# Decode attention on two kv heads at a time: 32 KB load rows, probabilities stationary, V moving

## The chip, the cores and the metric

The kernel runs on one core of a Trainium2 chip. The metric is the device time of one execution in microseconds (us). Two kernels are compared by the ratio of the mean time of one kernel's fast runs to the mean of the other's fast runs of the same rounds, so it is not quite the ratio of the medians that are quoted beside it. Traces and pages come from one profiled execution per kernel.

## The reference, cut to what matters

Eight sequences decode one token each through a modulated attention block and a gated feed-forward block. Nearly all bytes are the K and V caches: 8 x 4 kv heads x 8192 keys x 128 values in bfloat16, 2.1 MB for one K or V of one head, 134 MB in all. The weights add 51 MB.

```python
B, Hq, Hkv, Sk, Dh = 8, 32, 4, 8192, 128         # 8 query heads share a kv head
q = (h @ wq).reshape(B, 1, Hq, Dh)
scores = einsum('bhqd,bhkd->bhqk', q, repeat(k_cache, 8)) * Dh ** -0.5
p = softmax(scores)
o = einsum('bhqk,bhkd->bhqd', p, repeat(v_cache, 8))
x = x + ga * (o @ wo)        # then layernorm, gate and up, ReLU gate, down
```

## The kernel before

All loads go through one list in program order into an arena of nine slots of 2 MB (16 KB per partition). A load takes the next stretch of the arena when everything in it has been read in program order, and SyncE then waits on the chip for those reads:

```python
def pump():
    while stream:
        key, src, n = stream[0]
        lo = cursor[0] if cursor[0] + n <= NSLOT * SLOT else 0
        if P.unread("arena", lo, lo + n):
            return
        ...
        P.op("sp", lambda e, dst=dst, src=src: e.dma_start(dst, src), writes=[slot_r(lo, lo + n)], dma=True)
...
for n in range(N):           # 32 kv heads, one 2 MB load of K and one of V each
    load(("k", n), A_k_cache[n // G, n % G].rearrange("(p c) d -> p (c d)", p=128), SLOT)
    load(("v", n), A_v_cache[n // G, n % G].rearrange("(p c) d -> p (c d)", p=128), SLOT)
```

For each kv head VectorE transposes K in 32x32 blocks (four parts), TensorE makes the scores (QK, 16 matmuls of N = 512), the maximum of each query head is found, ScalarE takes the exponential, VectorE turns the probabilities, and TensorE multiplies with V. In this product V is the stationary operand and eight columns of probabilities move:

```python
for cc in range(NC):         # 64 matmuls of N = 8 per kv head
    fns.append(lambda e, cc=cc: e.matmul(ps[:, 3, col:col + J], vv[:, cc, :], pv_[:, cc % 16, cc // 16, :],
                                         start=(cc == 0), stop=(cc == NC - 1)))
```

The head loop is software-pipelined: K of head n+1 is transposed while the scores of head n and PV of head n-1 are made.

## Time and profile before

| | before |
|---|---|
| median time | 445.77 us (445.73 to 446.13, 4 runs) |
| span of the profiled run | 444.1 us |
| bytes read | 185.6 MB, 418 GB/s over the span |
| busy: PE, DVE, ACT | 66%, 49%, 7% |
| the last load has landed | 440.0 us |

How to read it: DMA engines are full in 38 of 40 slices while no compute engine is busy for more than two thirds of the time. So the question for any change is what it does to the stream of loads: how long a byte takes on its engine, and whether the engines always have a next load waiting. The lines are in the prediction.

### The profile page before, as it was taken

How to read it: one execution, taken by the hardware profiler on the slowest of the kernel's cores; microseconds unless marked ns; L12 is line 12 of the kernel's file. 1: busy time of each engine (PE TensorE's matmuls, PEld its weight loads, DVE VectorE, ACT ScalarE, POOL GpSimd, SP SyncE). 2: the span in 40 equal slices, each digit the busy share in tenths (PEclk: the TensorE clock that was granted, in tenths of full speed). 3: DMA queues.
4: the chain of work that ended last, by engine and by line, in shares of the span. 5: the costliest groups of instructions: out<-in, count | busy, mean ns of one | idle time of the engine just before them, and what ended most of it. 6: DMA issues, size and time to landing. Idle time of an engine off the chain costs nothing.

```text
span 444.1 us, 7822 instructions
## 1 busy us (share of the span) xinstructions
PE 290.9 (66%) x3514; PEld 165.4 (37%) x3514; DVE 217.7 (49%) x333; ACT 33.2 (7%) x78; POOL 30.8 (7%) x141
## 2 busy tenths in 40 slices
PE   0235355677858676776877767786777787558753
PEld 0111022344434333443433334343333345348741
DVE  0503065666655566666555566665556664230000
ACT  0200010000001000000100000001000002000000
POOL 4000020100000001000000110000001000000000
PEclk9995576887788888879688888778888869655555
DMA  8999999999999999999999999999999999999993
GB/s 344 421 428 425 434 434 428 426 429 437 427 428 432 431 426 426 435 434 425 426 434 429 425 429 435 429 425 432 429 430 428 429 421 403 422 430 429 426 429 151
DMA packets 16770, 186.14 MB, mean 419 GB/s; under 512 B 1537, under 2 KB 1633, under 8 KB 5985
## 3 DMA queue, kind: packets, MB, share of 16 engines
q1 hardware_dynamic: 16704, 185.64, 98.5%
q8 instruction: 27, 0.44, 0.4%
q14 instruction: 7, 0.05, 0.0%
q10 hardware_dynamic: 32, 0.01, 0.0%
HBM read 185.63 MB, written 0.02 MB: 418 GB/s over the span
## 4 chain that ended last, share of the span: by engine, by line
DMA 83%; PE 8%; DVE 7%; issue 1%; ACT 0%; SPq 0%; POOL 0%; DVEq 0%; ACTq 0%; POOLq 0%
DMA arena<-in_A_k_cache_dram 62%; DMA arena<-in_B_W_down_dram 8%; DMA arena<-in_A_wq_dram 7%; DMA arena<-in_A_wo_dram 4%; PE ps L460 4%; DVE kt L411 3%; DMA c_r<-in_c_dram 2%; PE ps L528 1%; DVE pT L450 1%; PE ps L334 1%; PE ps L420 1%; PE ps L357 0%; DVE lu L281 0%; ACT L278 0%; DVE hT L286 0%
## 5 line engine op out<-in xcount | busy, mean ns | idle before, releaser
L411 DVE STREAM_TRANSPOSE kt<-arena 128x1024 uint32<-128x1024 uint32 x128 | 153.3, 1218 | 114.6 <-DMA arena<-in_A_k_cache_dram 114.6
L420 PE MATMUL ps<-kt,qpad 128*128 128x512 bf16 x512 | 161.5, 482 | 2.0 <-POOL qpad L400 2.0
L420 PEld LDWEIGHTS ps<-kt,qpad 128*128 128x128 bf16 x512 | 60.9, 119 | 91.8 <-issue 60.6
L460 PE MATMUL ps<-pT,arena 128*128 128x8 bf16 x2048 | 56.0, 166 | 49.2 <-DVE pT L450 49.2
L460 PEld LDWEIGHTS ps<-pT,arena 128*128 128x128 bf16 x2048 | 54.1, 96 | 63.6 <-issue 63.3
L400 POOL COPY qpad<-qR 32x32 bf16<-32x32 bf16 x128 | 26.0, 203 | 312.8 <-PE ps L420 256.0
L430 PE MATMUL ps<-identf,negm 128*128 128x128 f32 x64 | 20.2, 408 | 37.0 <-DVE negm L426 37.0
L444 ACT ACTIVATE prb<-ps,bias 128x512 bf16<-128x512 f32 x32 | 22.0, 687 | 283.9 <-DVE mjt L438 283.9
L528 PE MATMUL ps<-hT,arena 128*128 128x8 bf16 x448 | 24.8, 194 | 7.7 <-DMA arena<-in_B_W_up_dram 3.0
L528 PEld LDWEIGHTS ps<-hT,arena 128*128 128x128 bf16 x448 | 24.4, 153 | 8.1 <-DMA arena<-in_B_W_up_dram 3.2
L430 PEld LDWEIGHTS ps<-identf,negm 128*128 128x128 f32 x64 | 12.3, 240 | 40.3 <-DVE negm L426 40.3
L450 DVE STREAM_TRANSPOSE pT<-prb 128x512 bf16<-128x512 bf16 x32 | 21.5, 672 | 1.7 <-ACT prb L444 1.7
L426 DVE TENSOR_REDUCE negm<-ps 128x1 f32<-128x512 f32 x32 | 20.9, 653 | 1.0 <-PE ps L420 1.0
L535 DVE TENSOR_TENSOR hmT<-ps,grel 128x224 bf16<-128x224 f32 x1 | 0.4, 391 | 30.7 <-ACT grel L533 30.7
L357 PE MATMUL ps<-arena,hT 128*32 128x512 bf16 x64 | 7.6, 627 | 11.2 <-DMA arena<-in_A_wq_dram 8.4
L303 PE MATMUL ps<-st,sel 128*128 128x1 f32 x4 | 1.2, 362 | 19.3 <-DVE st L302 19.3
L334 PE MATMUL ps<-arena,hT 128*32 128x512 bf16 x96 | 9.0, 544 | 6.8 <-DMA arena<-in_w_mod_dram 6.8
L545 PE MATMUL ps<-arena,hmT 128*32 128x256 bf16 x112 | 7.1, 415 | 7.4 <-DMA arena<-in_B_W_down_dram 7.4
L509 PE MATMUL ps<-arena,oT 128*32 128x256 bf16 x128 | 6.4, 382 | 5.2 <-DMA arena<-in_A_wo_dram 2.6
L341 DVE COPY mod<-ps 128x512 f32<-128x512 f32 x2 | 1.3, 670 | 15.2 <-PE ps L334 15.2
L436 DVE TENSOR_REDUCE mj<-ps 128x8 f32<-128x128 f32 x32 | 8.1, 252 | 1.2 <-PE ps L430 1.2
L303 PEld LDWEIGHTS ps<-st,sel 128*128 128x128 f32 x4 | 1.0, 310 | 19.6 <-DVE st L302 19.6
(64 smaller groups left out, 66.0 us busy)
## 6 DMA issues: line engine op xcount, KB each, us to landing
arena<-in_A_k_cache_dram SPq DMA_DIRECT2D x32, 2048.0 KB, 25.7
arena<-in_A_v_cache_dram SPq DMA_DIRECT2D x32, 2048.0 KB, 30.2
arena<-in_w_mod_dram SPq DMA_DIRECT2D x4, 3072.0 KB, 18.2
arena<-in_A_wq_dram SPq DMA_DIRECT2D x4, 2048.0 KB, 35.0
arena<-in_A_wo_dram SPq DMA_DIRECT2D x4, 2048.0 KB, 19.1
arena<-in_B_W_gate_dram SPq DMA_DIRECT2D x4, 1792.0 KB, 24.2
arena<-in_B_W_up_dram SPq DMA_DIRECT2D x4, 1792.0 KB, 28.0
arena<-in_B_W_down_dram SPq DMA_DIRECT2D x3, 1792.0 KB, 33.8
```

What stands on the lines that cost most here:

```text
L334: fns.append(lambda e, w=w, pr=pr, j=j, kk=kk: e.matmul(ps[32 * j:32 * j + 32, pr, :], hT[:, kk, :], w[:, 2 * pr:2 * pr + 2, j, :], start= ...
L357: fns.append(lambda e, w=w, z=z, g=g, kk=kk: e.matmul(ps[32 * g:32 * g + 32, 3 + z, :], hT[:, kk, :], w[:, g, z, :], start=(kk == 0), stop ...
L400: P.op("pool", lambda e, n=n, Q=Q: e.tensor_copy(qpad[32 * Q:32 * Q + 32, n % NQ, :, 24 + 32 * Q:32 + 32 * Q], qR[32 * Q:32 * Q + 32, :, n ...
L411: P.op("dve", lambda e: e.transpose(ktb[:, to:to + QE].bitcast(dt.uint32), arena[:, lo:lo + QE].bitcast(dt.uint32)), reads=[slot_r(lo, lo ...
L420: fns.append(lambda e, t=t, r=r: e.matmul(ps[:, n % 2, :].rearrange("p (c k) -> p c k", k=32), qpad[:, n % NQ, t * 2 + r, 24 - 8 * i:152 - ...
L426: P.op("dve", lambda e: e.tensor_reduce(negm[:, n % 2:n % 2 + 1], ps[:, n % 2, :], AX.X, ALU.max, negate=True), reads=[bank(n % 2)], write ...
L430: P.op("pe", lambda e: e.matmul(ps[:, 2, 0:128], negm[:, n % 2:n % 2 + 1].to_broadcast([128, 128]), identf[:], start=True, stop=True), rea ...
L436: P.op("dve", lambda e: e.tensor_reduce(mj[:, z, :], ps[:, 2, 0:128].rearrange("p (m j) -> p j m", j=J), AX.X, ALU.min), reads=[bank(2)], ...
L444: P.op("act", lambda e: e.activation(prb[:, z, :], ps[:, z, :], ACT.Exp, bias=bias[:, z:z + 1], scale=scale, accum_out=lall[:, n:n + 1]), ...
L450: P.op("dve", lambda e: e.transpose(pT[:, z, :], prb[:, z, :]), reads=[R("prb", z, z + 1)], writes=[R("pT", z, z + 1)])
L460: fns.append(lambda e, cc=cc: e.matmul(ps[:, 3, col:col + J], vv[:, cc, :], pv_[:, cc % 16, cc // 16, :], start=(cc == 0), stop=(cc == NC ...
L528: fns.append(lambda e, w=w, f=f, kk=kk, off=off, first=first: e.matmul(ps[:, 0, off + f * B:off + (f + 1) * B], w[:, f // FR, f % FR, :], ...
```

## The change

The intent is to handle two kv heads together: K and V of a pair come as one load of 4 MB with rows of 32 KB, half the partitions for each head. In PV the probabilities become the stationary operand (64 columns, zeros off the head's own block) and V moves with N = 512, in two column tiles side by side (matmuls that use one half each of TensorE's columns). The wanted 8-row diagonal blocks are then picked out and added by VectorE (the fold). The diff, cut to its core:

```diff
-        ktb = sb("kt", [128, 2 * SLOT], dt.bfloat16)
+        ktb = sb("kt", [128, 6 * 2048], dt.bfloat16)
-        for n in range(N):
-            load(("k", n), A_k_cache[n // G, n % G].rearrange("(p c) d -> p (c d)", p=128), SLOT)
-            load(("v", n), A_v_cache[n // G, n % G].rearrange("(p c) d -> p (c d)", p=128), SLOT)
+        for m in range(M):
+            for nm, t in (("k", A_k_cache), ("v", A_v_cache)):
+                load((nm, m), t[m // 2, 2 * (m % 2):2 * (m % 2) + 2].rearrange("g (p c) d -> (g p) (c d)", p=64), 2 * SLOT)
...
+            for t in range(32):
+                fns.append(lambda e, t=t: e.matmul(
+                    ps[64 * (t % 2):64 * (t % 2) + 64, 5, :].rearrange("p (i d) -> p i d", d=Dh),
+                    pT[:, z, t].rearrange("p g x -> p (g x)"), vv[:, t // 16, t % 16], start=(t < 2), stop=(t >= 30),
+                    tile_position=(0, 64 * (t % 2))))
...
+        def fold(m):
+            P.op("dve", lambda e: e.tensor_scalar(out=om[:], in0=ps[:, 5, 0:Dh], scalar1=im[:, 0:1], scalar2=None, op0=ALU.mult), ...)
+            for i in range(1, 4):
+                P.op("dve", lambda e, i=i: e.scalar_tensor_tensor(
+                    out=om[:], in0=ps[:, 5, Dh * i:Dh * i + Dh], scalar=im[:, i:i + 1], in1=om[:], op0=ALU.mult, op1=ALU.add), ...)
...
+        for m in range(M):
+            for e8 in range(8):
+                kt_part(m, e8)                       # K transpose of pair m, part e8
+                qk_part(m, e8)
+                if m >= 1:
+                    if e8 == 0:
+                        rowmax(m - 1, 1)
+                        spread(m - 1)
+                    elif e8 == 1:
+                        headmax(m - 1)
+                        expo(m - 1)
+                    elif e8 == 3:
+                        p_turn(m - 1)
+                    elif e8 == 4:
+                        pv(m - 1)
+                    elif e8 == 7:
+                        fold(m - 1)
+                if e8 == 5:
+                    rowmax(m, 0)
```

More of the change, by code (lines that the diff above doesn't have):

```diff
@@ L167, in bass_adaLN_cond__gqa_block_cached__glu_gated_reglu__decode_kernel @@
         sel = sb("sel", [128, 128], dt.float32)
-        jm = sb("jm", [128, J], dt.float32)
-        jms = sb("jms", [128, J], dt.float32)
+        jm = sb("jm", [128, 2, J], dt.float32)
+        jms = sb("jms", [128, 2 * J], dt.float32)
+        jmp = sb("jmp", [128, 2, J], dt.float32)
+        im = sb("im", [128, 4], dt.float32)
         c_r = sb("c_r", [128, 256], dt.bfloat16)
@@ L179, in bass_adaLN_cond__gqa_block_cached__glu_gated_reglu__decode_kernel @@
         qR = sb("qR", [128, 4, N, J], dt.bfloat16)
-        NQ = 3
-        qpad = sb("qpad", [128, NQ, 4, 152], dt.bfloat16)
-        prb = sb("prb", [128, 2, 512], dt.bfloat16)
-        pT = sb("pT", [128, 2, 512], dt.bfloat16)
-        negm = sb("negm", [128, 2], dt.float32)
-        mj = sb("mj", [128, 2, J], dt.float32)
-        mjt = sb("mjt", [128, J], dt.float32)
+        M = N // 2
+        qpad = sb("qpad", [128, 2, 4, 152], dt.bfloat16)
+        prb = sb("prb", [128, 1024], dt.bfloat16)
+        pT = sb("pT", [128, 2, 32, 2, 32], dt.bfloat16)
+        negm = sb("negm", [128, 4], dt.float32)
+        mj = sb("mj", [128, 2 * J], dt.float32)
+        mjt = sb("mjt", [128, 2 * J], dt.float32)
         bias = sb("bias", [128, 2], dt.float32)
-        lall = sb("lall", [128, N], dt.float32)
-        lx = sb("lx", [128, N, J], dt.float32)
+        lall = sb("lall", [128, M], dt.float32)
+        lx = sb("lx", [128, M, 2 * J], dt.float32)
+        om = sb("om", [128, Dh], dt.float32)
         oT = sb("oT", [128, Hq, 32], dt.bfloat16)
@@ L271, in bass_adaLN_cond__gqa_block_cached__glu_gated_reglu__decode_kernel @@
         P.op("pool", lambda e: e.memset(ones[:], 1.0), writes=[R("ones")])
-        P.op("pool", lambda e: e.memset(qpad[:], 0.0), writes=[R("qpad", 0, NQ)])
+        P.op("pool", lambda e: e.memset(qpad[:], 0.0), writes=[R("qpad", 0, 2)])
+        P.op("pool", lambda e: e.memset(pT[:], 0.0), writes=[R("pT", 0, 2)])
         P.op("pool", lambda e: e.memset(oT[:], 0.0), writes=[R("oT")])
@@ L291, in bass_adaLN_cond__gqa_block_cached__glu_gated_reglu__decode_kernel @@
              reads=[R("identf")], writes=[R("dsel")])
-        P.op("dve", lambda e: e.tensor_reduce(jm[:], identf[:].rearrange("p (m j) -> p j m", j=J), AX.X, ALU.add),
+        P.op("dve", lambda e: e.tensor_reduce(jm[:], identf[:].rearrange("p (g m j) -> p g j m", g=2, j=J), AX.X, ALU.add),
              reads=[R("identf")], writes=[R("jm")])
+        P.op("dve", lambda e: e.tensor_reduce(jmp[:], identf[:].rearrange("p (t g i j) -> p g j t i", t=2, g=2, j=J), AX.XY,
+                                              ALU.add), reads=[R("identf")], writes=[R("jmp")])
+        P.op("dve", lambda e: e.tensor_reduce(im[:], identf[:].rearrange("p (t i j) -> p i t j", t=4, j=J), AX.XY, ALU.add),
+             reads=[R("identf")], writes=[R("im")])
         P.op("dve", lambda e: e.tensor_scalar(out=sel[:].rearrange("p (q r) -> p q r", q=4),
@@ L296, in bass_adaLN_cond__gqa_block_cached__glu_gated_reglu__decode_kernel @@
                                               op0=ALU.mult), reads=[R("dsel")], writes=[R("sel")])
-        P.op("dve", lambda e: e.tensor_scalar(out=jms[:], in0=jm[:], scalar1=scale, scalar2=None, op0=ALU.mult),
+        P.op("dve", lambda e: e.tensor_scalar(out=jms[:], in0=jm[:].rearrange("p g j -> p (g j)"), scalar1=scale, scalar2=None, op0=ALU.mult),
              reads=[R("jm")], writes=[R("jms")])
@@ L393, in bass_adaLN_cond__gqa_block_cached__glu_gated_reglu__decode_kernel, with make_qpad, kt_part, qk_part @@
                              writes=[R("qR", u * 2 + jh, u * 2 + jh + 1)])
-        def make_qpad(n):
-            if n >= N:
+        QE = SLOT // 4
+        def make_qpad(m):
+            if m >= M:
                 return
             for Q in range(4):
-                P.op("pool", lambda e, n=n, Q=Q: e.tensor_copy(qpad[32 * Q:32 * Q + 32, n % NQ, :, 24 + 32 * Q:32 + 32 * Q],
-                                                             qR[32 * Q:32 * Q + 32, :, n, :]),
-                     reads=[R("qR", 0, 8)], writes=[R("qpad", n % NQ, n % NQ + 1)])
-        QE = SLOT // 4
-        def kt_part(n, i):
-            if n >= N:
-                return
-            lo = place["k", n] + i * QE
-            to = (n % 2) * SLOT + i * QE
+                P.op("pool", lambda e, n=2 * m + Q // 2, Q=Q: e.tensor_copy(
+                    qpad[32 * Q:32 * Q + 32, m % 2, :, 24 + 32 * Q:32 + 32 * Q], qR[32 * Q:32 * Q + 32, :, n, :]),
+                     reads=[R("qR", 0, 8)], writes=[R("qpad", m % 2, m % 2 + 1)])
+        def kt_part(m, e8):
+            lo = place["k", m] + e8 * QE
+            to = (8 * m + e8) % 6 * QE
             P.op("dve", lambda e: e.transpose(ktb[:, to:to + QE].bitcast(dt.uint32), arena[:, lo:lo + QE].bitcast(dt.uint32)),
                  reads=[slot_r(lo, lo + QE)], writes=[R("kt", to, to + QE)])
-        def qk_part(n, i):
-            to = (n % 2) * SLOT + i * QE
+        def qk_part(m, e8):
+            to = (8 * m + e8) % 6 * QE
+            i = e8 % 4
+            b = 2 * (m % 2) + e8 // 4
             kv = ktb[:, to:to + QE].rearrange("p (c t k r) -> p c t k r", t=2, k=32, r=2)
@@ L420, in qk_part @@
                     fns.append(lambda e, t=t, r=r: e.matmul(
-                        ps[:, n % 2, :].rearrange("p (c k) -> p c k", k=32), qpad[:, n % NQ, t * 2 + r, 24 - 8 * i:152 - 8 * i],
+                        ps[:, b, :].rearrange("p (c k) -> p c k", k=32), qpad[:, m % 2, t * 2 + r, 24 - 8 * i:152 - 8 * i],
                         kv[:, :, t, :, r], start=(i == 0 and t == 0 and r == 0), stop=(i == 3 and t == 1 and r == 1)))
-            P.op("pe", fns, reads=[R("kt", to, to + QE), R("qpad", n % NQ, n % NQ + 1)], writes=[bank(n % 2)])
@@ L425, in rowmax @@
-        def rowmax(n):
-            P.op("dve", lambda e: e.tensor_reduce(negm[:, n % 2:n % 2 + 1], ps[:, n % 2, :], AX.X, ALU.max, negate=True),
-                 reads=[bank(n % 2)], writes=[R("negm", n % 2, n % 2 + 1)])
-        def spread(n):
-            P.op("pe", lambda e: e.matmul(ps[:, 2, 0:128], negm[:, n % 2:n % 2 + 1].to_broadcast([128, 128]), identf[:],
-                                         start=True, stop=True), reads=[R("negm", n % 2, n % 2 + 1), R("identf")],
-                 writes=[bank(2)])
@@ L434, in headmax @@
-        def headmax(n):
-            z = n % 2
-            P.op("dve", lambda e: e.tensor_reduce(mj[:, z, :], ps[:, 2, 0:128].rearrange("p (m j) -> p j m", j=J), AX.X, ALU.min),
-                 reads=[bank(2)], writes=[R("mj", z, z + 1)])
-            P.op("dve", lambda e: e.scalar_tensor_tensor(out=mjt[:], in0=mj[:, z, :], scalar=1.0, in1=jms[:], op0=ALU.mult,
-                                                         op1=ALU.mult, accum_out=bias[:, z:z + 1]),
-                 reads=[R("mj", z, z + 1), R("jms")], writes=[R("mjt"), R("bias", z, z + 1)])
@@ L442, in expo @@
-        def expo(n):
-            z = n % 2
-            P.op("act", lambda e: e.activation(prb[:, z, :], ps[:, z, :], ACT.Exp, bias=bias[:, z:z + 1], scale=scale,
-                                               accum_out=lall[:, n:n + 1]),
-                 reads=[bank(z), R("bias", z, z + 1)], writes=[R("prb", z, z + 1), R("lall", n, n + 1)])
-        def p_turn(n):
-            z = n % 2
-            P.op("dve", lambda e: e.transpose(pT[:, z, :], prb[:, z, :]), reads=[R("prb", z, z + 1)],
-                 writes=[R("pT", z, z + 1)])
@@ L453, in pv @@
-        def pv(n):
-            z = n % 2
-            col = n * J
-            fns = []
-            vv = arena[:, place["v", n]:place["v", n] + SLOT].rearrange("p (c d) -> p c d", d=Dh)
-            pv_ = pT[:, z, :].rearrange("p (c i j) -> p c i j", i=4, j=J)
-            for cc in range(NC):
-                fns.append(lambda e, cc=cc: e.matmul(ps[:, 3, col:col + J], vv[:, cc, :], pv_[:, cc % 16, cc // 16, :],
-                                                     start=(cc == 0), stop=(cc == NC - 1)))
-            P.op("pe", fns, reads=[slot_r(place["v", n], place["v", n] + SLOT), R("pT", z, z + 1)], writes=[bank(3)])
+            P.op("pe", fns, reads=[R("kt", to, to + QE), R("qpad", m % 2, m % 2 + 1)], writes=[bank(b)])
@@ new lines, in rowmax, with spread @@
+        def rowmax(m, h):
+            b = 2 * (m % 2) + h
+            P.op("dve", lambda e: e.tensor_reduce(negm[:, h:h + 1], ps[:, b, :], AX.X, ALU.max, negate=True),
+                 reads=[bank(b)], writes=[R("negm", h, h + 1)])
+        def spread(m):
+            P.op("dve", lambda e: e.tensor_tensor(out=negm[:, 2:3], in0=negm[:, 0:1], in1=negm[:, 1:2], op=ALU.min),
+                 reads=[R("negm", 0, 2)], writes=[R("negm", 2, 3)])
+            P.op("pe", lambda e: e.matmul(ps[:, 4, 0:128], negm[:, 2:3].to_broadcast([128, 128]), identf[:],
+                                         start=True, stop=True), reads=[R("negm", 2, 3), R("identf")], writes=[bank(4)])
@@ new lines, in headmax @@
+        def headmax(m):
+            z = m % 2
+            P.op("dve", lambda e: e.tensor_reduce(mj[:].rearrange("p (g j) -> p g j", g=2),
+                                                  ps[:, 4, 0:128].rearrange("p (g m j) -> p g j m", g=2, j=J), AX.X, ALU.min),
+                 reads=[bank(4)], writes=[R("mj")])
+            P.op("dve", lambda e: e.scalar_tensor_tensor(out=mjt[:], in0=mj[:], scalar=1.0, in1=jms[:], op0=ALU.mult,
+                                                         op1=ALU.mult, accum_out=bias[:, z:z + 1]),
+                 reads=[R("mj"), R("jms")], writes=[R("mjt"), R("bias", z, z + 1)])
@@ new lines, in expo, with p_turn @@
+        def expo(m):
+            z = m % 2
+            P.op("act", lambda e: e.activation(prb[:], ps[:, 2 * z:2 * z + 2, :].rearrange("p h n -> p (h n)"), ACT.Exp,
+                                               bias=bias[:, z:z + 1], scale=scale, accum_out=lall[:, m:m + 1]),
+                 reads=[bank(2 * z, 2), R("bias", z, z + 1)], writes=[R("prb"), R("lall", m, m + 1)])
+        def p_turn(m):
+            z = m % 2
+            for g in range(2):
+                P.op("dve", lambda e, g=g: e.transpose(pT[64 * g:64 * g + 64, z, :, g, :], prb[64 * g:64 * g + 64, :]),
+                     reads=[R("prb"), R("pT", z, z + 1)], writes=[R("pT", z, z + 1)])
@@ new lines, in pv @@
+        def pv(m):
+            z = m % 2
+            lo = place["v", m]
+            vv = arena[:, lo:lo + 2 * SLOT].rearrange("p (h i c d) -> p h c i d", h=2, i=4, d=Dh)
+            fns = []
+            for t in range(32):
[3 more added lines that the diff above has]
+                    tile_position=(0, 64 * (t % 2))))
+            P.op("pe", fns, reads=[slot_r(lo, lo + 2 * SLOT), R("pT", z, z + 1)], writes=[bank(5)])
@@ new lines, in fold @@
+        def fold(m):
+            P.op("dve", lambda e: e.tensor_scalar(out=om[:], in0=ps[:, 5, 0:Dh], scalar1=im[:, 0:1], scalar2=None, op0=ALU.mult),
+                 reads=[bank(5), R("im")], writes=[R("om")])
+            for i in range(1, 4):
+                P.op("dve", lambda e, i=i: e.scalar_tensor_tensor(
+                    out=om[:], in0=ps[:, 5, Dh * i:Dh * i + Dh], scalar=im[:, i:i + 1], in1=om[:], op0=ALU.mult, op1=ALU.add),
+                     reads=[bank(5), R("im"), R("om")], writes=[R("om")])
+            P.op("pe", lambda e: e.matmul(ps[:, 6, 16 * m:16 * m + 16], om[:], jmp[:].rearrange("p g j -> p (g j)"),
+                                         start=True, stop=True), reads=[R("om"), R("jmp")], writes=[bank(6)])
@@ L464, in bass_adaLN_cond__gqa_block_cached__glu_gated_reglu__decode_kernel @@
         make_qpad(0)
         make_qpad(1)
-        for i in range(4):
-            kt_part(0, i)
-        for n in range(N):
-            kt_part(n + 1, 0)
-            if n >= 1:
-                p_turn(n - 1)
-            kt_part(n + 1, 1)
-            qk_part(n, 0)
-            qk_part(n, 1)
-            qk_part(n, 2)
-            qk_part(n, 3)
-            kt_part(n + 1, 2)
-            if n >= 1:
-                pv(n - 1)
-            rowmax(n)
-            kt_part(n + 1, 3)
-            spread(n)
-            headmax(n)
-            expo(n)
-            make_qpad(n + 2)
@@ L486, in bass_adaLN_cond__gqa_block_cached__glu_gated_reglu__decode_kernel @@
-        p_turn(N - 1)
-        pv(N - 1)
-        P.op("dve", lambda e: e.tensor_tensor(out=lx[:], in0=lall[:, :, None].to_broadcast([128, N, J]),
-                                              in1=jm[:, None, :].to_broadcast([128, N, J]), op=ALU.mult),
-             reads=[R("lall", 0, N), R("jm")], writes=[R("lx")])
+        for m in range(M):
[17 more added lines that the diff above has]
+                    rowmax(m, 0)
+            make_qpad(m + 2)
@@ new lines, in bass_adaLN_cond__gqa_block_cached__glu_gated_reglu__decode_kernel @@
+        rowmax(M - 1, 1)
+        spread(M - 1)
+        headmax(M - 1)
+        expo(M - 1)
+        p_turn(M - 1)
+        pv(M - 1)
+        fold(M - 1)
+        P.op("dve", lambda e: e.tensor_tensor(out=lx[:], in0=lall[:, :, None].to_broadcast([128, M, 2 * J]),
+                                              in1=jm[:].rearrange("p g j -> p (g j)")[:, None, :].to_broadcast([128, M, 2 * J]),
+                                              op=ALU.mult),
+             reads=[R("lall", 0, M), R("jm")], writes=[R("lx")])
@@ L497, in bass_adaLN_cond__gqa_block_cached__glu_gated_reglu__decode_kernel @@
         P.op("dve", lambda e: e.tensor_tensor(out=oT[:, :, 0:B],
-                                              in0=ps[:, 3, 0:N * J].rearrange("p (b h) -> p h b", b=B),
+                                              in0=ps[:, 6, 0:N * J].rearrange("p (b h) -> p h b", b=B),
                                               in1=lr.rearrange("p (b h) -> p h b", b=B), op=ALU.mult),
-             reads=[bank(3), R("lx"), R("oT")], writes=[R("oT")])
+             reads=[bank(6), R("lx"), R("oT")], writes=[R("oT")])
         for q in range(4):
```

## The prediction

> **What bounds the kernel now.** I read the page first: the slices and queues, then the chain that ended last.
>
> ```profile
> span 444.1 us, 7822 instructions
> ...
> PEclk9995576887788888879688888778888869655555
> DMA  8999999999999999999999999999999999999993
> ...
> q1 hardware_dynamic: 16704, 185.64, 98.5%
> q8 instruction: 27, 0.44, 0.4%
> ...
> DMA 83%; PE 8%; DVE 7%; issue 1%; ACT 0%; SPq 0%; POOL 0%; DVEq 0%; ACTq 0%; POOLq 0%
> ```
>
> The 16 DMA engines are full in all slices but the first and the last, and 83% of the last-ending chain is DMA. Next, the chain in order of time, in the middle of attention:
>
> ```profile
> 187.73 1.82 PE ps L460 x64
> 189.55 0.02 issue
> 189.57 25.27 DMA arena<-in_A_k_cache_dram
> 214.84 0.02 issue
> 214.86 1.25 DVE kt L411
> 216.11 0.60 DVE pT L450
> ```
>
> Columns are start, length, what. PV frees a slot at 189.55, the next K load goes out, and lands 25.3 us later, behind five others in the queue. A period of 29.1 us (187.73 to 216.85, the next PV) carries three heads, six loads of 2.097 MB: 432 GB/s. So this is a full queue, not a latency loop. The windows say the same:
>
> ```profile
> 28.00:52.00 24.00, 8.44 (x72) 2.20 (x72) 3.39 (x7) 0.60 (x1) 0.00 (x0) 0.57 1.01 432
> 180.00:240.00 60.00, 44.47 (x495) 24.18 (x496) 38.03 (x56) 4.67 (x12) 4.87 (x24) 0.80 1.01 430
> 371.00:387.00 16.00, 10.24 (x229) 8.29 (x227) 4.51 (x8) 2.06 (x3) 0.00 (x0) 0.68 1.05 413
> 434.00:440.00 6.00, 2.97 (x52) 1.52 (x52) 0.00 (x0) 0.00 (x0) 0.00 (x0) 0.50 0.52 214
> ```
>
> (Window, then busy time of PE, PE weight load, DVE, ACT, POOL; the last three are granted clock, DMA share, GB/s.) K and V run at 430 GB/s with 16 KB rows, wq at 432 with 16 KB rows, wo with 2 KB rows at 413. In the last 6 us the engines finish one after another. In attention DVE is busy 38 of 60 us, PE 44, so neither binds.
>
> **What the Trainium skill says.** "DMA: Bandwidth & Descriptors", section "Where 436 GB/s comes from", puts the ceiling at 435.2 GB/s. The trace agrees: 430 to 432 sustained, so a better descriptor can win at most 1.2% of the K and V time. The same page, "Why small descriptors are slow", gives a fixed overhead per packet. The trace's list of single packets shows it: typically 84 ns for 2 KB, 535 for 14 KB, 611 for 16 KB, 912 for 24 KB. From the last two, 8192 B cost 301 ns (27.2 GB/s per engine), leaving 611 - 602 = 9 ns fixed; 2 KB checks as 75 + 9 = 84. "TensorEngine Tiling (Array Packing)", "Key Properties", says that column tiles run in parallel. wq's matmuls do, four tiles of 32 columns:
>
> ```profile
> 43.11 1.90 PE L357 MATMUL ps<-arena,hT 128*32 128x512 bf16 x16 [2.26 <-DMA arena<-in_A_wq_dram]
> ```
>
> 119 ns each, where single matmuls of N = 512 are modelled by "TensorE: Matmul & The Clock Gate" ("Back-to-back issue gap") as N/1.2 ns = 427 cold and 216 warm. The QK group agrees: 16 in 3.64 us warm (228 each).
>
> **The change, part by part.** Durations are from these rows:
>
> ```profile
> L411 DVE STREAM_TRANSPOSE kt<-arena 128x1024 uint32<-128x1024 uint32 x128 | 153.3, 1218 | 114.6 <-DMA arena<-in_A_k_cache_dram 114.6
> L444 ACT ACTIVATE prb<-ps,bias 128x512 bf16<-128x512 f32 x32 | 22.0, 687 | 283.9 <-DVE mjt L438 283.9
> L450 DVE STREAM_TRANSPOSE pT<-prb 128x512 bf16<-128x512 bf16 x32 | 21.5, 672 | 1.7 <-ACT prb L444 1.7
> L426 DVE TENSOR_REDUCE negm<-ps 128x1 f32<-128x512 f32 x32 | 20.9, 653 | 1.0 <-PE ps L420 1.0
> ```
>
> *On the path, DMA.* Bytes stay. 8192 packets of 16 KB become 4096 of 32 KB, so 4096/16 x 9 ns = 2.3 us less per engine. 32 fewer DMAs save 32 completion writes per engine at 9 ns, 0.3 us. PV goes from 2048 to 512 matmuls, each with a weight load: 3072 fewer instructions of 7822, so some 10 of the 27 instruction packets go, 10 x 0.61/16 = 0.4 us. Sum: 3.0 us less.
>
> *Beside the path, PE.* QK keeps 32 matmuls per pair of heads, 32 x 216 = 6.9 us warm, 13.7 cold. PV per pair was 2 x 64 small ones, 2 x 1.75 = 3.5 us. Now it is 32 of N = 512 on two column tiles: 16 x 216 = 3.5 us warm, 6.8 cold. It is equal when warm. All warm, a pair takes 6.9 + 3.5 + 0.8 for the spread and the fold's small product = 11.2 us.
>
> *Beside the path, DVE, per pair.* Eight K transposes 9.7, two row maxima 1.3, the minimum and the head maximum 0.7. The turn of P has two instructions of 64 partitions x 1024, each as long as the 1024-wide K transpose: 2.4, where two at 672 were 1.3. The fold has four reads of 128 PSUM columns, an estimate of 0.3 each from the 252 ns of the head maximum over 128 columns: 1.2. Sum 15.3 us. A pair is 8.39 MB, 19.5 us at 430 GB/s. DVE still fits, rising from 13.1 of 19.5 us to 15.3.
>
> *Buffers: the thing to check.* Loads are now 4.2 MB (9.75 us). Four double slots alternate, and the ninth slot lies idle in most of attention. When K(m) lands at T, only V(m) and K(m+1) are queued, 19.5 us of work. V(m+1) needs the slot of V(m-1), free when PV(m-1) ends. I add up DVE's order: first transpose 1.25, row maximum and minimum to 2.1, second transpose to 3.3, head maximum after the spread to 4.4, two transposes to 6.8 (exp, 687 + 512 x 0.83 = 1.1 us and its accumulator read, fits beside), the turn of P to 9.3, fifth transpose to 10.5. PE then does the fifth QK part, to 11.4 warm or 12.2 cold, and PV, to 14.9 warm or 19.1 cold. A tiny DMA costs 2.3 us from issue to the end (the output: 441.75 to 444.1). So the load is in time if PV ends before T + 17.2. Warm it does by 2.3 us, fully cold it misses by 1.9. The granted clock is now 0.80 in this stage; QK parts come densely from T + 1.3, so I expect PV mostly warm, near T + 15.5, and no gap.
>
> *Tail.* After the last V lands (X), 30.4 MB or 70.8 us of weights follow. Before, the last PV ended at 377.1 with the last V at about X = 368.5 (30.4 MB before 439.7): X + 8.6. Now a whole pair is processed after its K: loop 15 ends about 18 to 19 us after K(15), at X + 9; row maximum, spread, exp, turn, PV and fold add 11 to 14; the ones product, reciprocal (1.76) and scaling 4: the scaled attention output is ready at about X + 24 to 27, where it was at X + 12. Wo (7.1), layernorm (6.4 as before) and 448 gate/up matmuls at 54 ns (24.4) take it to X + 61.9 to 64.9; the gating and the down matmuls (1 + 6 us) to X + 68.9 to 71.9. The loads end at X + 71. So DMA and PE nearly tie: 0 to 1 us lost, 0.5 expected. No load waits in between: wo and the first two gates and ups cover until X + 36.6, while PV(15) ends by X + 23.
>
> **The rivals.** *Starved queue.* If PV ends at T + p with p over 17.2, two pairs take at least p + 2.3 + 19.5 us. Each us too late costs 0.5 us per pair, some 7 us over 14 pairs; fully cold 1.9 x 7 = 13 us, or 459. For it: the clock swings between 0.5 and 1, and slack falls from 25 us of queued loads to about 2. Against: PV stays as short as before when warm, and PE wants 11.2 of 19.5 us. I give it 0.2. *Compute binds.* If column tiles do not overlap, PV alone takes 6.9 us warm and 13.7 cold, and DVE waits in the fold: p = 18.3 warm, 450 or more. Against it is the wq row, 119 ns. 0.1, within the 0.2. *No gain from descriptors.* If 32 KB rows cost two 16 KB packets, only 0.4 us is left, and the tail eats it: 446. *Better than counted.* If K and V reached 435.2 GB/s, 312 us would be 308.4, 3.6 less, and the last 6 us, where the engines' finishes spread, could shrink too: 439 to 440.
>
> **Range and chances.** 445.8 - 3.0 + 0.5 = 443.3. The gain is capped near 440; the loss has a longer side through the starved queue, so 440 to 453. Two per cent is 436.9 or 454.7. Below 436.9 the bytes at 435.2 GB/s (426.6 us) plus start and end (3 + 4.4) leave almost no room: 0.02. Above: 0.08.
>
> **What would show it.** Right: packets of about 1213 ns for 32 KB, 432 to 433 GB/s in attention, DMA share full, DVE's largest wait still for K, PV at about 110 ns per matmul, and fewer instruction packets. Wrong: SP waiting for PV with holes in the DMA share (starved), fold waiting for PV while K lies ready (compute), PE busy without a gap from the wo product to the end, with the last down load landed long before (tail).

## The result

The changed kernel took 450.94 us median (450.68 to 454.43, 4 runs) against 445.77 us before: ratio 1.0132, 95% interval 1.0083 to 1.0182. It is 1.3% slower, within the stated range, but on the other side of the kernel before than the point of 443.3 us. The profiled run of the changed kernel is the 454.43 us one, the slowest of the four; all are of the fast state.

The page of the changed kernel, the lines that answer to those of before:

```profile
span 452.6 us, 4601 instructions
...
PEclk9985559596879879889889988689988898686555
DMA  8999999999999999999999998999999999999994
GB/s 350 428 418 434 439 434 436 426 421 423 410 426 379 445 411 397 412 381 438 411 427 388 440 434 381 411 379 436 431 429 435 433 376 379 418 427 433 428 424 203
...
q1 hardware_dynamic: 12096, 185.64, 97.5%
q8 instruction: 15, 0.25, 0.2%
...
DMA 48%; PE 24%; DVE 22%; issue 5%; SPq 1%; ACT 0%; POOL 0%; POOLq 0%
```

The DMA row looks as full as before; a digit 9 hides up to a tenth. The GB/s row does not: in attention it drops again and again below 400, where it stayed at 425 or more before. And the chain is now half compute. The chain in order of time shows how:

```profile
176.92 3.59 PE ps L472 x32
180.51 0.02 issue
180.54 0.36 DVE om L479
180.90 0.00 issue
180.90 23.71 DMA arena<-in_A_k_cache_dram
204.62 0.02 issue
204.64 1.25 DVE kt L418
...
215.26 5.28 PE ps L472 x32
220.54 0.03 issue
220.57 0.36 DVE om L479
220.93 0.00 issue
220.93 23.22 DMA arena<-in_A_k_cache_dram
```

K of a pair lands at 204.6, and PV, which frees the slot of the next V load, ends at 220.5, 15.9 us later. The V load goes out at 220.56 and the next K load behind it at 220.93 (the chain names the K, the one that ends last). In windows, columns as in the prediction:

```profile
183.00:200.00 17.00, 11.26 (x51) 4.45 (x52) 13.36 (x16) 1.20 (x2) 0.81 (x4) 0.80 1.00 431
200.00:204.00 4.00, 3.69 (x22) 1.67 (x18) 1.40 (x4) 0.00 (x0) 0.33 (x2) 1.00 0.94 344
204.00:221.00 17.00, 11.16 (x57) 4.47 (x58) 13.76 (x18) 1.21 (x2) 0.48 (x3) 0.90 1.00 430
221.00:225.00 4.00, 2.36 (x13) 1.14 (x10) 1.42 (x4) 0.00 (x0) 0.81 (x4) 1.00 0.87 328
```

Seventeen us at 430 GB/s, then four at 328 to 344: each of these two late releases is followed by a hole. Over 180 to 240 us it comes to 409 GB/s. The trace's packet list shows it more sharply, as the mean number of packets in flight in each us (16 engines, so 16 is full):

```
us     200    201    202    203    204  ...  220    221    222    223    224
       16.1   12.9   12.3   15.3   16.0      16.1   15.7   14.5   15.1   16.0
```

The same list gives a ledger. Busy is the packets' time divided by 16 engines, idle the rest up to the end of the last load. (Records of successive packets overlap by a few ns, so idle can come out just below zero.)

```
                     last load ends   busy    idle   mean K/V packet   engines' spread at the end
before                    440.0      439.3     0.7     613 ns (16 KB)           5.9 us
changed                   448.6      442.3     6.2    1240 ns (32 KB)           3.2 us
```

The spread is the time from the first to the last of the 16 engines' completions of one of the last loads. Two things were lost: engines stand idle for 5.5 us more, and the average 32 KB packet takes 1240 ns although the typical one takes 1213. The slow ones sit at the holes: the slowest packet after each one takes 2.1 to 2.8 us.

### The profile page after: what moved, and what is told of

The parts are those of the page before. It is cut to its first block, busy times and chain, and to the rows that moved or that the text cites. A ratio compares the mean times of both kernels' runs of the same rounds, so it can differ in the third digit from the quotient of the medians.

```text
span 452.6 us, 4601 instructions
## 1 busy us (share of the span) xinstructions
PE 281.5 (62%) x1978; PEld 132.3 (29%) x1978; DVE 257.7 (57%) x367; ACT 27.6 (6%) x46; POOL 20.7 (5%) x78
## 4 chain that ended last, share of the span: by engine, by line
DMA 48%; PE 24%; DVE 22%; issue 5%; SPq 1%; ACT 0%; POOL 0%; POOLq 0%
DMA arena<-in_A_k_cache_dram 35%; PE ps L472 11%; DVE kt L418 11%; PE ps L429 7%; DMA arena<-in_w_mod_dram 6%; DMA arena<-in_B_W_down_dram 6%; DVE pT L463 6%; PE ps L558 2%; PE ps L539 1%; DVE negm L436 1%; PE ps L342 1%; DVE mj L447 1%; PE ps L442 1%; SPq L261 0%; DVE om L479 0%
## 5 line engine op out<-in xcount | busy, mean ns | idle before, releaser
L429 PE MATMUL ps<-kt,qpad 128*128 128x512 bf16 x512 | 147.6, 429 | 106.4 <-DVE kt L418 61.9
L429 PEld LDWEIGHTS ps<-kt,qpad 128*128 128x128 bf16 x512 | 47.2, 104 | 190.3 <-DVE kt L418 89.7
L472 PE MATMUL ps<-arena,pT 128*64 128x512 bf16 x512 | 73.4, 451 | 4.5 <-DVE pT L463 4.5
L472 PEld LDWEIGHTS ps<-arena,pT 128*64 128x64 bf16 x512 | 32.6, 129 | 46.3 <-issue 30.6
L463 DVE STREAM_TRANSPOSE pT<-prb 64x1024 bf16<-64x1024 bf16 x32 | 39.0, 1220 | 1.8 <-ACT prb L456 1.3
L456 ACT ACTIVATE prb<-ps,bias 128x1024 bf16<-128x1024 f32 x16 | 17.8, 1113 | 291.8 <-DVE mjt L450 291.8
L411 POOL COPY qpad<-qR 32x32 bf16<-32x32 bf16 x64 | 13.0, 203 | 322.7 <-PE ps L429 270.2
L479 DVE TENSOR_SCALAR om<-ps,im 128x128 f32<-128x128 f32 x16 | 5.6, 351 | 33.1 <-PE ps L472 33.1
L482 DVE SCALAR_TENSOR_TENSOR om<-ps,im,om 128x128 f32<-128x128 f32 x48 | 16.8, 351 | 1.7
L442 PE MATMUL ps<-identf,negm 128*128 128x128 f32 x32 | 7.9, 338 | 0.8 <-DVE negm L440 0.8
## 6 DMA issues: line engine op xcount, KB each, us to landing
arena<-in_A_v_cache_dram SPq DMA_DIRECT2D x16, 4096.0 KB, 14.2
arena<-in_A_wo_dram SPq DMA_DIRECT2D x4, 2048.0 KB, 19.4
```

The source lines that it names most:

```text
L411: P.op("pool", lambda e, n=2 * m + Q // 2, Q=Q: e.tensor_copy(qpad[32 * Q:32 * Q + 32, m % 2, :, 24 + 32 * Q:32 + 32 * Q], qR[32 * Q:32 * ...
L429: fns.append(lambda e, t=t, r=r: e.matmul(ps[:, b, :].rearrange("p (c k) -> p c k", k=32), qpad[:, m % 2, t * 2 + r, 24 - 8 * i:152 - 8 * ...
L442: P.op("pe", lambda e: e.matmul(ps[:, 4, 0:128], negm[:, 2:3].to_broadcast([128, 128]), identf[:], start=True, stop=True), reads=[R("negm" ...
L456: P.op("act", lambda e: e.activation(prb[:], ps[:, 2 * z:2 * z + 2, :].rearrange("p h n -> p (h n)"), ACT.Exp, bias=bias[:, z:z + 1], scal ...
L463: P.op("dve", lambda e, g=g: e.transpose(pT[64 * g:64 * g + 64, z, :, g, :], prb[64 * g:64 * g + 64, :]), reads=[R("prb"), R("pT", z, z + ...
L472: fns.append(lambda e, t=t: e.matmul(ps[64 * (t % 2):64 * (t % 2) + 64, 5, :].rearrange("p (i d) -> p i d", d=Dh), pT[:, z, t].rearrange(" ...
```

## The experiments

State of the theories before them. **Starved queue** (the prediction's first rival): the next V load is released so late that engines run dry, although not as late as the prediction thought necessary. Rival 1: 32 KB packets are slower by themselves (mean 1240 ns). Rival 2: the time is lost in the tail, where the attention output is ready 24 us after the last V. All kernels here gave correct results.

### One slot more, and its control

```diff
-    NSLOT = 9
+    NSLOT = 10                                     # only in the first kernel, not in the control
-        ktb = sb("kt", [128, 6 * 2048], dt.bfloat16)
+        ktb = sb("kt", [128, 4 * 2048], dt.bfloat16)
-        pT = sb("pT", [128, 2, 32, 2, 32], dt.bfloat16)
+        pT = sb("pT", [128, 1, 32, 2, 32], dt.bfloat16)
-        ob = sb("ob", [128, 256], dt.bfloat16)
+        ob = hb
```

> The changed kernel with ten slots instead of nine (room made by a K ring of four parts, one pT buffer, and the output written into an old tile), so that five 4 MB loads fit and a third load is queued when a K lands. Theory (starved queue): the holes in the DMA share and the slow first packets after them go; of 450.9 us the 8 us of them are won back, 442 to 443.5 us, packets of 32 KB at 1213 ns in the mean within 1%. Rival 1 (32 KB packets are themselves slower, 1240 ns in the mean): 449 to 451. Rival 2 (the time is lost in the tail, where the attention output is ready 24 us after the last V): 449 to 451.

Measured: 442.57 us median (442.42 to 442.75, 6 runs) against 446.58 for the kernel before on the same chip, ratio 0.9914 (0.9899 to 0.9929). (The kernel before has two groups of fast runs, 445.6 to 446.2 and 446.6 to 447.6 us; the four runs of the first round are all of the lower one.) The window of the same 60 us in which the changed kernel moved 409 GB/s:

```profile
180.00:240.00 60.00, 40.46 (x206) 17.09 (x207) 45.41 (x64) 3.62 (x6) 2.45 (x12) 0.89 1.00 432
```

There is no hole left, the mean 32 KB packet takes 1214 ns, and the last load ends at 436.6 us. V loads now go out 3 to 5 us before the K of the pair ahead of them lands, instead of 14 to 16.5 us after it.

> The control for the ten-slot kernel: nine slots as in the changed kernel, with the same smaller K ring, one pT buffer and shared output tile. All theories: as the changed kernel, 450 to 452 us, with the same holes. If it is faster by more than 1 us, the ten-slot result is not due to the slots alone.

Measured: 452.02 us (449.38 to 453.0, 6 runs), ratio 1.0117, as the changed kernel; mean packet 1240 ns and idle 4.6 us. So the smaller buffers do nothing, and the slot is worth 9.5 us. Rival 1 falls, because the same 32 KB packets are fast when the queue is never empty. Rival 2 falls, because the tail keeps its order of work.

### PV earlier, with nine slots

```diff
-                    elif e8 == 3:
-                        p_turn(m - 1)
-                    elif e8 == 4:
-                        pv(m - 1)
+                    elif e8 == 2:
+                        p_turn(m - 1)
+                        pv(m - 1)
```

> The changed kernel with the turn of P after the third instead of the fourth K transpose and PV right behind it, ahead of two QK parts; nine slots, 32 KB. PV should end about 3 us earlier, near 12.5 to 13 us after K lands instead of 15.9. Theory (starved queue): the next V load is issued before the engines run dry, most holes close, 442.5 to 445 us. Rival 1 and rival 2: 449.5 to 451.

Measured: 442.42 us (442.32 to 442.67, 5 runs), ratio 0.9913 (0.9897 to 0.9928). From the timeline of this kernel, VectorE's, TensorE's and SyncE's lines of one pair (start, length, engine, line, what):

```profile
199.35 1.25 DVE L418 STREAM_TRANSPOSE kt<-arena 128x1024 uint32<-128x1024 uint32 x1 [2.75 <-DMA arena<-in_A_k_cache_dram]
...
207.47 3.64 PE L472 MATMUL ps<-arena,pT 128*64 128x512 bf16 x32 [1.19 <-DVE pT L463]
...
211.14 0.33 SPq L231 DMA_DIRECT2D arena<-in_A_v_cache_dram  x1
```

PV ends and the V load goes out 11.8 us after the K landed, a little earlier than expected. In flight are 16.0 to 16.1 packets in every us from 198 to 222. No buffer was added and no instruction saved: the order of four lines was worth 8.5 us. It is as fast as the ten-slot kernel and beats both kernels of the study.

### Both remedies

The ten-slot kernel with the early PV.

> Both remedies, ten slots and the early PV. Theory: each alone already closes the holes, so there is nothing left to win: 442.2 to 442.7 us. If each remedy had closed only part of the loss, both together would be at 441.5 or less.

Measured: 442.66 us (442.53 to 442.74, 4 runs), ratio 0.9919. Each remedy alone had closed the holes; together they win nothing more.

### A longer PV, with nine and with ten slots

```diff
+            more = [lambda e, t=t: e.matmul(ps[64 * (t % 2):64 * (t % 2) + 64, 7, :]..., start=True, stop=True,
+                    tile_position=(0, 64 * (t % 2))) for t in range(16)]
-            P.op("pe", fns, reads=[..., R("pT", z, z + 1)], writes=[bank(5)])
+            P.op("pe", more + fns, reads=[..., R("pT", z, z + 1)], writes=[bank(5), bank(7)])
```

> The changed kernel (nine slots) with 16 extra PV matmuls per pair into a scratch bank, ahead of the 32, so that V is held 1.8 us (warm) to 3.4 us longer: PV ends near 17.7 to 19 us after K lands. Theory (starved queue): every us of a later V release costs half a us per pair; with the loss of 8.4 us over some 14 pairs at 15.9 us, the onset is near 14.7, and 17.7 to 18.5 costs 21 to 27 us in all: 461 to 470 us. If the queue were not the cause, 16 more matmuls beside idle time of PE cost under 1 us: 450 to 452.

Measured: 459.18 us (455.2 to 460.73, 4 runs), a little below the expected 461 to 470. V loads go out 16 to 18.3 us after the K lands.

> The ten-slot kernel with the same 16 extra PV matmuls. Theory: the third queued load covers it, and PE has the time: 442.5 to 445 us. If the extra matmuls cost time for another reason (PE or the fold on VectorE, which waits for PV), it loses as much as the nine-slot kernel does.

Measured: two runs at 442.94 and 443.98 us, two at 452.04 and 453.78, which count as slow because they lie over 1.5% above the fastest; the verdict of 0.9937 is from the fast ones. Their times fit a third load that covers the longer PV, as expected, but no trace of a fast run was kept. The granted clock was 0.840 and 0.843 in the fast runs, 0.818 and 0.800 in the slow ones. The profile fell on the 453.78 us run: pairs come every 20.4 us in it instead of 19.4, and PE works on until 448.5 although the last load has landed at 440. As it is of the slow state, no cause is read from it.

The nine-slot kernel with the longer PV does have a fast profile (455.2 us, the fastest of its four). There the fold waits longer for PV than in the changed kernel, which is the second line (who waits, for whom, us in all, times, longest):

```profile
DVE om L483 <- PE ps L472: 61.1, 16, 7.7
```

```profile
DVE om L479 <- PE ps L472: 33.1, 16, 5.4
```

VectorE still waits for K in 14 of the 16 pairs (35.9 us in all). So this pair of kernels does not separate cleanly. The fast runs agree with the theory; but a PV this long can also bind through the fold, the prediction's second rival, and part of the nine-slot kernel's 459 may be that. Why a run of the ten-slot version falls on one side or the other stays open.

### 16 KB loads that release halves

```diff
+                for a in range(2):
+                    load((nm, m, a), t[...].rearrange("g (p c) d -> (g p) (c d)", p=64)[:, a * SLOT:(a + 1) * SLOT], SLOT)
-            lo = place["k", m] + e8 * QE
+            lo = place["k", m, e8 // 4] + e8 % 4 * QE
+            for a in range(2):                    # PV in two operations of 16 matmuls, one per half of V
```

> The changed kernel's arithmetic, but each K and V of a pair loaded as two 2 MB loads with 16 KB rows into single slots, and each half released when its four transposes or its 16 PV matmuls are done; all nine slots are in use. Theory (starved queue): no holes; 16 KB packets at 611 ns; 444.5 to 446 us, near the kernel before, as only fewer instruction packets remain of the gain. Rival 1 (32 KB packets slow): also about 445. Rival 2 (tail): 449 to 451, as the tail keeps its order of work.

Measured: 443.84 us (443.71 to 443.99, 6 runs), ratio 0.9944 (0.993 to 0.9957), a little below the expected 444.5 to 446. It has the kernel before's packets, in number and size, and the changed kernel's arithmetic, and is already 2.7 us below the before of this round (446.58 us), or 2 below the 445.8 of the first. It lies 1.3 us above the ten-slot kernel. So the gain has two parts, and the next runs measure each.

### Descriptor size alone

First attempt: the ten-slot kernel with the access pattern of each load split into two pieces per row.

```diff
-                load((nm, m), t[...].rearrange("g (p c) d -> (g p) (c d)", p=64), 2 * SLOT)
+                load((nm, m), t[...].rearrange("g (p c) d -> (g p) (c d)", p=64).rearrange("p (a n) -> p a n", a=2), 2 * SLOT)
```

> The ten-slot kernel with each 32 KB row sent as two descriptors of 16 KB in the same DMA; nothing else changes. It measures the descriptor size alone. As the prediction counted it (9 ns per packet, 256 fewer per engine) it should be 2.3 us slower than with 32 KB rows: 444.9. If successive packets of one engine overlap by about 4.5 ns, as the packet records suggest (mean number in flight 16.12 with 16 KB, 16.05 with 32 KB), only 1.2 us: 443.7.

Measured: 442.62 us, which says nothing on descriptors: the packet list still had 4096 packets of 32 KB. The split had not reached the packets. It is a repeat of the ten-slot kernel, and agrees with it to 0.05 us. Second attempt: two DMAs for each load.

```diff
-                P.op("sp", lambda e, dst=dst, src=src: e.dma_start(dst, src), writes=[slot_r(lo, lo + n)], dma=True)
+                for a in range(0, n, SLOT) if n == 2 * SLOT else (0,):
+                    ...                            # d1, s1: columns a to a + SLOT of dst and src
+                    P.op("sp", lambda e, dst=d1, src=s1: e.dma_start(dst, src), writes=[slot_r(lo + a, lo + a + w)], dma=True)
```

> The ten-slot kernel with each 4 MB load sent as two DMAs of 2 MB, one per half of the rows, so that the packets really are of 16 KB (the version with a split access pattern still ran as 4096 packets of 32 KB and took 442.62 us, so it tested nothing). If a packet costs the 9 ns of the prediction, 2.3 us slower than with 32 KB, 444.9; if successive packets overlap by half of it, 1.2 us slower, 443.8, as the half-load kernel's 443.84 suggests; if descriptor size is worth nothing, 442.6.

Measured: 443.93 us (443.8 to 444.01, 5 runs), ratio 0.9948. The 32 KB rows are worth 1.3 to 1.4 us, half of what the packets' durations alone say. The list says why: with 16 KB packets 16.11 are in flight in a full stretch, with 32 KB 16.05. An engine starts its next packet before the last one is off the books, and 0.11/16 of 611 ns is 4 ns, about half of the 9 ns that the prediction charged to each packet.

### Instructions alone

The ten-slot kernel with 3072 more instructions in PE's idle time, as many as the change removed.

```diff
+        def idle_mm(k):
+            P.op("pe", [lambda e: e.matmul(ps[:, 7, 0:8], identb[:], identb[:, 0:8], start=True, stop=True)] * k,
+                 reads=[R("identb")], writes=[bank(7)])
...
+                if e8 in (3, 7):
+                    idle_mm(48)
```

> The ten-slot kernel with 96 tiny matmuls per pair (N = 8, from an SBUF constant into an unused bank, no data), 48 in each of the two idle stretches of PE: 3072 more instructions, as many as the change took out. If instruction loads are what the other gain came from (27 instruction packets before, 15 after, and engines that drift apart by them), it takes about 12 more instruction packets, ends with the engines 5 to 6 us apart instead of 3.8, and is 1 to 2 us slower: 443.6 to 444.6. If instruction loads do not matter, 442.6 as without them (PE has idle time for them).

Measured: 445.38 us (444.3 to 445.46, 14 runs), ratio 0.9971 (0.9961 to 0.998): 2.8 us slower than without them, more than expected. (Five of the 14 runs lie at 444.3 to 444.8, the other nine, with the profiled one, at 445.4: 1.9 or 2.8 us slower.) From its page and its last windows, against the ten-slot kernel's last 6 us of loads:

```profile
q8 instruction: 27, 0.44, 0.4%
...
434.00:440.00 6.00, 3.54 (x56) 1.67 (x56) 0.00 (x0) 0.00 (x0) 0.00 (x0) 0.50 0.32 130
```

```profile
431.00:437.00 6.00, 3.34 (x52) 1.56 (x52) 0.00 (x0) 0.00 (x0) 0.00 (x0) 0.50 0.60 244
```

PE waits for the loads there in both. There are 27 instruction packets again, as before the change, and in the last 6 us the engines are one third busy instead of six tenths: the 16 engines finish 6.8 us apart instead of 3.8. A load has landed when the last of its 16 completions has come, so the last engine sets the end. The packet list has each instruction packet at 16 KB and 0.93 us in the mean. The 12 extra ones would cost 0.7 us if they were spread evenly over 16 engines; in the profiled run they move the end by 2.8. That they fall on a few engines is inferred from the spread, as the trace does not name a packet's engine. It grows in steps that fit: instruction packets start at 181.2 and 195.1 us, and the spread of the landings goes from 2.5 us (179.8) to 3.3 (190.3) and 4.0 (200.7).

The ledger of all this, as above:

```
                     last load ends   busy    idle   mean K/V packet   spread at the end
ten slots                 436.6      435.5     1.0    1214 ns (32 KB)        3.8 us
early PV                  436.7      435.6     1.1    1214 ns (32 KB)        3.8 us
half loads                437.8      438.1    -0.3     612 ns (16 KB)        3.8 us
two DMAs                  437.8      438.2    -0.4     612 ns (16 KB)        3.8 us
more instructions         439.4      436.6     2.7    1216 ns (32 KB)        6.8 us
```

## Why the prediction was right or wrong

**What bounds the kernel: right.** It was and is the stream of loads. Every version without holes that was profiled in a fast run ends 4.1 to 4.2 us after its last load has landed.

**Work of the engines beside the path: right, but for the fold.** The rows of the changed kernel:

```profile
L418 DVE STREAM_TRANSPOSE kt<-arena 128x1024 uint32<-128x1024 uint32 x128 | 152.8, 1224 | 57.8 <-DMA arena<-in_A_k_cache_dram 57.3
L472 PE MATMUL ps<-arena,pT 128*64 128x512 bf16 x512 | 73.4, 451 | 4.5 <-DVE pT L463 4.5
L463 DVE STREAM_TRANSPOSE pT<-prb 64x1024 bf16<-64x1024 bf16 x32 | 39.0, 1220 | 1.8 <-ACT prb L456 1.3
L456 ACT ACTIVATE prb<-ps,bias 128x1024 bf16<-128x1024 f32 x16 | 17.8, 1113 | 291.8 <-DVE mjt L450 291.8
```

The turn of P takes 1220 ns per instruction (predicted as the 1218 of the K transpose), the exponential 1113 (1.1 us). The mean of 451 ns in the PV row is of overlapped matmuls; the chain has 32 of them in 3.59 us when warm (granted clock 1.00) and 5.28 in a mixed clock (0.68), 112 and 165 ns each, where 110 was predicted. So the two column tiles do run side by side. A fold step takes 351 ns, not 300.

**The release of V: the time right, the deadline wrong. This is the step that failed.** "So the load is in time if PV ends before T + 17.2." PV ends 14.2 to 16.5 us after K lands, most often at 15.9, close to "near T + 15.5"; and yet the engines run dry. The 17.2 was 19.5 us of queued work less 2.3 us for a tiny DMA. The mis-sized term is the first. T is when the last of the 16 engines has landed its share of K. Of the 16 completions of the K that lands at 204.62, the first came at 201.78 and the 14th at 202.50; the engine that finished first has 2.8 us less to do than T says. For the 12 K loads of this trace whose completions can be told apart, the first and the last are 1.8 to 4.8 us apart, as much as the whole margin. The trace of the kernel before already showed 1.5 to 4.6 us. The second term was not too small: the packets of a new load start 1.0 to 1.5 us after its issue. An estimate of the real deadline for this K is 19.4 - 2.8 - 1.4 = 15.2 us after T, where 1.4 is the time from the issue at 220.56 to the first slow packet of the new load at 221.97.

The changed kernel's trace brackets it. Of its V loads from 118.9 us on, the three that went out 14.2 to 14.5 us after T leave no hole; of the ten at 14.9 to 16.5, nine are followed by 0.2 to 1.2 us of idle time, as a mean over the engines. In the kernel with the longer PV, where the completions of a K are only 0.6 to 2.1 us apart, releases at 16.0 to 16.2 us still leave none to speak of (at most 0.03 us), and in the early-PV kernel, with releases at 11.3 to 11.8 us, there is none. So the deadline moves with the spread of the engines, as the estimate says.

What the prediction left out is the price of a miss. The load issued at 220.56 has all engines at work again only at 224, and its first packets take up to 2.35 us instead of 1.21. Each hole also costs more than its idle time: against the ten-slot kernel the profiled run of the changed kernel, its slowest, has 5.2 us more idle and 6.8 us more packet time, 12.0 us in its last load's end.

**The chance of it: too small.** The first rival was named with its mechanism and its sign in the profile, SyncE waiting for PV and holes in the rate, and was given 0.2 on the strength of a margin of 2 us that did not exist.

**The gain: the sum nearly right by luck, its terms wrong.** Counted: 2.3 us for packets, 0.3 for completions, 0.4 for instruction loads, 3.0 in all. Measured without the holes: 1.3 to 1.4 for the first two together (two DMAs against one), and 1.9 to 2.8 for the fewer instructions (half loads against before, which differ in the arithmetic too; more instructions against ten slots). The 0.61 us that the prediction took for an instruction packet is that of a 16 KB data packet; the list has 0.93, and the larger part of the cost goes with the engines' drift apart, which the prediction did not count. The two errors largely cancel: the ten-slot and the early-PV kernel are at 442.4 to 442.6 us, 3.2 us under the 445.8 of the first round and 4.0 to 4.2 under the 446.58 of their own. So 443.3 would have been nearly right for a kernel that differs in the order of four lines.

**The tail: right.** The attention output was due at X + 24 to 27 and is ready at 399.7, 24.2 us after the last V landed at 375.5. PE's gate and up matmuls start at 411 and hide behind the loads; the chain ends with a down load from 420.54 to 448.24. The half us set aside for the tail was not needed.

## What to carry to other kernels

When a kernel lives on a full load queue, count the slack from the engine that finishes first and not from the semaphore that fires last: here they were 1.8 to 4.8 us apart, and a margin of 2 us was none. A miss costs more than the wait, as the engines were all at work again only 3.4 us after the late load went out. Larger loads in the same arena are fewer loads in flight: here the better descriptor was worth 1.3 us, and the slack that it took cost 8.5. Before buying buffers, move the work that frees the buffer earlier: it did the same for nothing.

## What the Trainium skill lacked or had wrong

- "Runtime: NRT & Kernel Launch", section "Instruction fetch mechanics", calls the cost of crossing a 16 KiB block of instructions "mostly hidden". In this kernel, which is bound by loads, it was not: with 3072 more instructions in PE's idle time the instruction packets went from 15 to 27, the time rose by 1.9 to 2.8 us, and the last engine finished 6.8 us behind the first instead of 3.8.
- "DMA: Bandwidth & Descriptors", "Why small descriptors are slow", explains the fixed overhead per packet but has no figure for rows of many KB. Packet durations here show 9 ns, and 4 to 5 ns of it overlap with the next packet: 16 KB against 32 KB rows is 443.93 against 442.57 us for 134 MB.
- The same page, section "Where 436 GB/s comes from", says that for transfers between HBM and SBUF the HBM side (about 358 GB/s) binds. With one core at work the trace of the kernel before holds 429 to 430 GB/s from 60 to 360 us. The same page's own table of loads by one core (425 GB/s for 16 MB) fits the trace; that sentence does not.
- No page that I read says how much must stay queued for the engines not to run dry. Here 19.4 us of work at the moment a load's semaphore fires was used up for the first engines about 15 to 17 us later, and the slowest packet after a hole took 2.1 to 2.8 us instead of 1.21.
